# Far-row products as extra matmul columns, near tables from SBUF, and output weights applied last, in a fused attention and convolution kernel

## The chip, the cores and the metric

The kernel runs on one core of a Trainium2 chip. The core has a matrix engine (TensorE, PE, with its weight loads as PEld), a vector engine (VectorE, DVE), a scalar engine with function tables (ScalarE, ACT), a small general engine (GpSimd, POOL), and queues that start DMA transfers, nearly all of them on SyncE (SP). SBUF is the working memory of 128 partitions; PSUM is the memory of eight banks into which PE writes its sums. The metric is the device time of one execution in microseconds; lower is better.

## The reference

Two independent halves are put side by side in the output. Half A is linear attention with 16 heads of 28 features, on 2048 rows of width 448. Half B is a long convolution of a signal `u` (2048 x 448) with a kernel made of 256 complex exponentials for each channel.

```python
# A
q, k, v = split(x @ wqkv)                                # 16 heads of 28
phi_q = concat(softmax(q @ w_phi), softmax(-(q @ w_phi)))  # the same for k
kv, z = phi_k^T @ v, sum(phi_k)
a = ((phi_q @ kv) / (phi_q . z + 1e-6)) @ wo
# B
dt = exp(log_dt);  P = exp(dt * (A_re + 1j*A_im) * l)    # l = 0..2047, rounded to bf16
K = real(sum_n C * P * dt * B)                           # (448, 2048)
y = irfft(rfft(u, 4096) * rfft(K, 4096))[:2048] + u * Dskip
out = concat([a, y], axis=-1)
```

## The kernel before, in words

The kernel first builds a list of about a thousand operations (`Prog.add`), each for one engine: E is PE, A is ACT, V is DVE, G is GpSimd, S is SP. Four lists written into the file then settle everything else. `ORDER` gives the order in which the operations are issued, and so the order on each engine; `PLACES` gives each buffer its address in SBUF; `SLOTS` gives each matmul group its PSUM banks; `PICKS` says for each movable copy, scaling or square (`either`, line 200) whether ACT or DVE does it. Each engine works strictly in its order. Nothing is chosen at run time.

**Half B** is worked on in four quarters `qt` of 112 channels. Because l is rounded to bf16, only 640 different positions l occur, and each is a high part `HI` (16 values, step 16) plus a low part `LO` (40 values). `tables(qt)` (line 789) makes the powers of the exponentials: `rotations` (sines and cosines) and `dampings` (exponentials) take their angles from PSUM, where `args` (line 454) has multiplied them by 1, 3, 5 and 7 on PE; `damp` multiplies the two into 14 near rows of the table `W`; `far` (line 499) makes the 24 far rows out of the near ones by complex products with the 256th power (`step`: two products, one difference, one sum) and by squaring (`squares`); `hi_tables` makes the table `U_` of the high parts by repeated complex products. `build_k` (line 552) then forms the kernel at all positions by matmuls of `U_` (32 columns of weights, four column groups side by side) with `W` (80 moving columns), and `scatter_k` brings the result into the layout of the spectrum by a round trip through DRAM (`KTd`).

The spectrum of the signal is made by `signal_spectrum` (line 406) for two blocks of 1024 rows. It needs the sum and the difference of the even rows and the reversed odd rows; the reversal is a matmul with `REV`, copied out of PSUM. `kernel_spectrum` does the same for the kernel; its second block also takes the first block's result (`sk0`) as a moving operand, and its copy out of PSUM permutes the columns. `conv(qt)` multiplies the spectra (`prod`, on DVE), adds up real and imaginary parts either on DVE (`finish`) or on PE (`finish_pe`, for the blocks named in `ON_PE`), and goes back by `inverse` (line 764): four groups of nine matmuls of 112 columns in a bank, one of the nine for Dskip, then a copy and a store.

**Half A**: `key_side` (line 594) forms exponentials of the keys for 8 pairs of row blocks, their sums (`bz`), reciprocals, the weighted values `VR` and the products `kv`; at its end it transposes `kv` and multiplies it with the output weights `wo` into `M`. `query_side(sc)` (line 637), four times, forms the queries' exponentials, the denominators, scales the exponentials with them and multiplies with `M` (eight matmuls for each 128 rows).

A few helpers issue almost everything, so most rows of the profile carry a helper's line: 177 is any two-operand DVE instruction, 194 a reciprocal, 198 an activation with a function, 205 a copy, 208 a scaling, 211 and 212 a square, 220 a matmul, 230 a transpose, 240 a DMA, 236 a DMA with transpose.

## Time and profile before

| | |
|---|---|
| runs shown, us | 238.6, 238.61, 236.22; median 238.6 |
| span of the profiled execution | 233.5 us |
| between the span and a run's time | 2.7 to 5.1 us; the profiled execution's own time is not shown apart from its span |
| PE busy | 208.1 us (89%), 3044 matmuls |
| DVE busy | 216.8 us (93%), 267 instructions |
| ACT busy | 183.9 us (79%), 321 instructions |
| POOL busy | 4.6 us |
| DMA | 36.4 MB in 81640 packets |

A busy time is that in which at least one instruction of the engine is under way; instructions of one engine overlap a little, so the sum of their durations is larger. Matmuls are pipelined, and a busy PE is not PE at its peak. The granted clock of TensorE was 1.000 over the span.

### The profile page before, as it was taken

The page shows a single profiled execution, that of the slowest core. Times are in us where ns is not written, and L with a number is a line of the kernel's source. Part 1 is how long each engine was busy: PE and PEld are TensorE (multiplying, and loading weights), DVE is VectorE, ACT ScalarE, POOL GpSimd, SP SyncE. Part 2 cuts the span into 40 slices and gives each one's busy share as a digit, 9 for nine tenths or more (in the row PEclk, how much of TensorE's full clock was granted, in tenths as well). Part 3 has the DMA queues.
Part 4 walks back from the last instruction along what each step waited for, and adds up shares of the span by engine and source line. Part 5 has one row for each costly group of instructions (what it writes and reads, how often), then busy time and mean ns, then how long its engine had stood idle before and what let it go on. Part 6 is the DMA issues. An engine that isn't in the chain of part 4 may idle for free.

```text
span 233.5 us, 7103 instructions
## 1 busy us (share of the span) xinstructions
PE 208.1 (89%) x3044; PEld 152.8 (65%) x3044; DVE 216.8 (93%) x267; ACT 183.9 (79%) x321; POOL 4.6 (2%) x20
## 2 busy tenths in 40 slices
PE   1173899998999999999987999999999999999994
PEld 1161446564557655589765678885579968689993
DVE  1799999999999999989999979999999999999980
ACT  3999999999999999999998998698328451355331
POOL 4000000000000100000000000000000000000000
PEclk9999999999999999999999999999999999999999
DMA  5999910499239999826865899872696890489643
GB/s 154 237 218 272 151 37 1 167 150 235 71 59 190 147 176 257 152 71 155 206 156 144 99 255 225 226 114 61 70 368 131 199 277 10 63 185 242 121 100 81
DMA packets 81640, 36.40 MB, mean 156 GB/s; under 512 B 65480, under 2 KB 79688, under 8 KB 81224
## 3 DMA queue, kind: packets, MB, share of 16 engines
q1 hardware_dynamic: 81368, 35.71, 73.3%
q8 instruction: 24, 0.39, 0.7%
q10 hardware_dynamic: 240, 0.23, 0.3%
q14 instruction: 8, 0.07, 0.1%
HBM read 19.44 MB, written 8.62 MB: 120 GB/s over the span
## 4 chain that ended last, share of the span: by engine, by line
PE 51%; ACT 17%; DVE 13%; DMA 5%; issue 3%; SPq 0%; ACTq 0%
PE psum L220 51%; DVE sbuf L177 11%; ACT sbuf L198 8%; ACT sbuf L205 7%; DMA sbuf<-sbuf 3%; DMA sbuf<-KTd 2%; ACT L198 1%; DVE sbuf L205 1%; DVE sbuf L194 0%; ACT sbuf L211 0%; SPq L240 0%; DVE sbuf L212 0%; ACT sbuf L208 0%; DVE sbuf L208 0%; PE psum L230 0%
## 5 line engine op out<-in xcount | busy, mean ns | idle before, releaser
L220 PE MATMUL psum<-sbuf 128*128 128x112 bf16 (+9 forms) x3000 | 206.2, 252 | 21.4 <-ACT sbuf L205 7.8
L177 DVE TENSOR_TENSOR sbuf<-sbuf 128x896 bf16<-128x896 bf16 (+11 forms) x222 | 197.3, 956 | 7.2 <-ACT sbuf L198 4.3
L220 PEld LDWEIGHTS <-sbuf 128*128 128x128 bf16 (+3 forms) x3000 | 150.1, 114 | 75.3 <-issue 18.2
L205 ACT CAST sbuf<-psum 128x448 bf16<-128x448 f32 (+4 forms) x129 | 79.7, 672 | 38.0 <-PE psum L220 37.3
L198 ACT ACTIVATE sbuf<-psum 128x448 bf16<-128x448 f32 (+4 forms) x110 | 65.5, 721 | 0.5 <-PE psum L220 0.4
L211 ACT ACTIVATE sbuf<-sbuf 128x896 bf16<-128x896 bf16 x14 | 14.2, 1024 | 4.0 <-DVE sbuf L177 4.0
L198 ACT ACTIVATE sbuf<-psum,sbuf 128x896 f32<-128x896 f32 (+3 forms) x17 | 13.6, 835 | 0.0
L208 ACT ACTIVATE sbuf<-sbuf 128x896 bf16<-128x896 bf16 (+2 forms) x10 | 10.9, 1091 | 1.4 <-DVE sbuf L299 0.8
L198 ACT ACT_TABLE_LOAD x8 | 10.3, 1283 | 1.4 <-PEq L900 1.3
L205 ACT COPY sbuf<-sbuf 128x224 bf16<-128x224 bf16 (+2 forms) x18 | 8.9, 512 | 0.0
L205 DVE CAST sbuf<-psum 128x448 bf16<-128x448 f32 (+3 forms) x8 | 5.3, 690 | 2.3 <-PE psum L220 1.7
L215 POOL MEMSET sbuf<- 128x224 bf16 (+4 forms) x15 | 4.2, 314 | 153.3 <-PE psum L220 153.1
L205 ACT COPY sbuf<-psum 112x896 bf16<-112x896 bf16 (+2 forms) x13 | 6.8, 549 | 0.1
L177 DVE TENSOR_TENSOR sbuf<-psum,sbuf 128x448 bf16<-128x448 f32 (+3 forms) x12 | 5.1, 444 | 0.1
L194 DVE RECIPROCAL sbuf<-psum 128x64 bf16<-128x64 f32 x8 | 4.3, 546 | 0.4 <-ACT sbuf L198 0.3
L230 PEld LDWEIGHTS <-sbuf 112*112 112x112 bf16 (+1 forms) x44 | 3.1, 128 | 1.8 <-DVE sbuf L177 0.8
L230 PE MATMUL psum<-sbuf 112*112 112x112 bf16 (+1 forms) x44 | 3.6, 215 | 0.6 <-DVE sbuf L177 0.6
L212 DVE TENSOR_TENSOR sbuf<-sbuf 128x896 bf16<-128x896 bf16 (+1 forms) x3 | 3.3, 1087 | 0.0
L194 DVE RECIPROCAL sbuf<-sbuf 128x64 f32<-128x64 f32 x4 | 2.2, 545 | 0.0
L189 DVE SCALAR_TENSOR_TENSOR sbuf<-sbuf 128x64 f32<-128x64 f32 (+1 forms) x5 | 2.0, 393 | 0.0
L205 ACT CAST sbuf<-sbuf 128x1792 bf16<-128x1792 f32 x1 | 1.8, 1814 | 0.0
L208 DVE TENSOR_SCALAR sbuf<-sbuf 128x1568 bf16<-128x1568 bf16 (+1 forms) x3 | 1.6, 538 | 0.0
(8 smaller groups left out, 2.1 us busy)
## 6 DMA issues: line engine op xcount, KB each, us to landing
SUd<-sbuf SPq DMA_DIRECT2D x8, 448.0 KB
sbuf<-SCd SPq DMA_DIRECT2D x16, 224.0 KB
sbuf<-SUd SPq DMA_DIRECT2D x4, 896.0 KB
sbuf<-const SPq DMA_DIRECT2D x3, 1024.0 KB
sbuf<-const SPq DMA_DIRECT2D x8, 384.0 KB
sbuf<-in_B_u_dram SPq DMA_DIRECT2D x4, 448.0 KB
out_dram<-sbuf SPq DMA_DIRECT2D x4, 448.0 KB
out_dram<-sbuf SPq DMA_DIRECT2D x16, 112.0 KB
```

The lines of the kernel that those rows point to most:

```text
L177: prog.add("V", lambda: nc.vector.tensor_tensor(out=o, in0=a, in1=b, op=op))
L189: prog.add("V", lambda: nc.vector.scalar_tensor_tensor(out=o, in0=a, scalar=s, in1=b, op0=op0, op1=op1))
L194: nc.vector.reciprocal(o, a)
L198: prog.add("A", lambda: nc.scalar.activation(o, a, fn, **kw))
L205: either(lambda: nc.scalar.copy(o, a), lambda: nc.vector.tensor_copy(o, a))
L208: either(lambda: nc.scalar.activation(o, a, ACT.Copy, scale=s), lambda: nc.vector.tensor_scalar_mul(o, a, s))
L211: either(lambda: nc.scalar.activation(o, a, ACT.Square), lambda: nc.vector.tensor_tensor(out=o, in0=a, in1=a, op=ALU.mult))
L212: lambda: nc.vector.tensor_tensor(out=o, in0=a, in1=a, op=ALU.mult))
L215: prog.add("G", lambda: nc.gpsimd.memset(o, v))
L220: nc.tensor.matmul(o, lhsT=l, rhs=r, **kw)
L230: nc.tensor.transpose(o, i, idn)
```

## The change

- **Near tables.** The angles stay in SBUF in fp32, in one part instead of two bf16 parts; `args` is gone. `rotations` and `dampings` issue 14 activations of 224 columns each, with the multiple as the activation's scale.
- **Far rows.** A complex product of a far row is split in two: the products with the real part are written to the far row, and the products with the imaginary part are written to one of 12 new rows of `W` (40 to 51, `X`) as they are. `build_k` takes 104 moving columns instead of 80, and one addition at the end of `tables` adds the two results. Three of the first seven far rows and two of the next four are still added up on DVE. The squares lose the factor two, which `GROWN` puts into the constant table of the spectrum.
- **High tables.** The last step adds the two products of the imaginary part at once instead of one difference and one sum.
- **Reciprocals** are Ln followed by Exp(-x) on ACT, from a table that holds both; ACT loads that table wherever it goes from sines to exponentials.
- **Signal.** `turn_u` writes the odd rows in reversed order to DRAM (`URd`), from where `load_u` reads them; the reversal matmuls and their copies are gone.
- **Column order.** The signal matmuls read their moving operand in permuted order, the copy of the kernel spectrum is plain, and the inverse writes its 112 columns permuted to PSUM (every other element, in runs of seven).
- **Output weights last.** `M` is gone; a query multiplies with `kv` into a numerator (`NT`, four groups of two matmuls of 512 columns), copies it, and multiplies with `wo` (four matmuls for each 128 rows).
- The second block of quarter 2 sums on PE as well (`ON_PE`).
- `ORDER`, `PLACES`, `SLOTS` and `PICKS` are new from beginning to end.

```diff
 N_LO = 40
 N_HI = 16
+N_W = 52
 QC = 224
 NCOL = 4 * QC
-ODD = [1, 3, 5, 7]
-LO = [0, 8] + [s * p for p in (2, 4, 6, 1, 3, 5, 7) for s in (-1, 1)]
-LO += [256 + p for p in LO[0:8]]
-LO += [2 * LO[i] for i in (16, 18, 19, 21)]
+MULT = (6, 4, 2, 3, 1, 5, 7)
+LO = [0, 8] + [s * p for p in MULT for s in (-1, 1)]
+LO += [256 + LO[i] for i in (0, 7, 6, 5, 4, 3, 2, 1)]
+LO += [2 * LO[i] for i in (16, 17, 18, 19)]
 LO += [256 + p for p in LO[24:28]]
-LO += [2 * LO[i] for i in (24, 26, 28, 30)]
+LO += [2 * LO[i] for i in (24, 25, 28, 29)]
...
+GROWN = [1, 1, 1, 2, 8]
+ON_PE = [(0, 1), (1, 1), (2, 1)]
...
+            F[blk, kt, r] += GROWN[kt] * np.stack([even.real, odd.real, even.imag, odd.imag])
...
-    def recip(o, a):
-        def fn():
-            with nc.allow_low_precision(reason="bf16 softmax weights, as in the reference"):
-                nc.vector.reciprocal(o, a)
-        prog.add("V", fn)
+    def recip(o, a, ln):
+        af(ln, a, ACT.Ln)
+        af(o, ln, ACT.Exp, scale=-1.0)
 
     def af(o, a, fn, **kw):
-        prog.add("A", lambda: nc.scalar.activation(o, a, fn, **kw))
+        def do():
+            kind = {ACT.Sin: "sin", ACT.Exp: "exp", ACT.Ln: "exp"}.get(fn)
+            if kind == "exp" and prog.kind != "exp":
+                nc.scalar.preload_act_table_set("natural_log_exp_and_others")
+            prog.kind = kind or prog.kind
+            nc.scalar.activation(o, a, fn, **kw)
+        prog.add("A", do)
 
...
+    ue = [sb([128, 4, D_MODEL]) for _ in range(2)]
+    uo = [sb([128, 4, D_MODEL]) for _ in range(2)]
+
+    def turn_u():
         rs = u2.ap[0][0]
-        return bass.AP(tensor=u2.tensor, offset=u2[row + 128 * (1 - a), 0].offset,
-                       ap=[[2 * rs, 64], [256 * rs, 4], [1, 2 * D_MODEL]])
-
-    ua = [sb([128, 4, 2, D_MODEL]) for _ in range(2)]
+        dma("S", URd.rearrange("(g i) d -> g i d", g=16),
+            bass.AP(tensor=u2.tensor, offset=u2[127, 0].offset, ap=[[128 * rs, 16], [-2 * rs, 64], [1, D_MODEL]]))
 
     def load_u(b):
+        rs = u2.ap[0][0]
         for a in range(2):
-            dma("S", ua[b][64 * a:64 * a + 64].rearrange("p t r d -> p t (r d)"), row_pairs(1024 * b, a))
+            p = slice(64 * a, 64 * a + 64)
+            dma("S", ue[b][p], bass.AP(tensor=u2.tensor, offset=u2[1024 * b + 128 * (1 - a), 0].offset,
+                                       ap=[[2 * rs, 64], [256 * rs, 4], [1, D_MODEL]]))
+            src = URd[64 * (8 * b + 6 + a), 0:1]
+            dma("S", uo[b][p], bass.AP(tensor=src.tensor, offset=src.offset,
+                                       ap=[[D_MODEL, 64], [-128 * D_MODEL, 4], [1, D_MODEL]]))
 
...
-            sub(o1, i, o0)
+            copy(view(dst[:, 56 * nch:56 * nch + 1], [112, 8], [1, 2], [2, 28]),
+                 view(psum[:, b[nch], 0:1], [56, 8], [28, 2], [1, 28]))
...
-        ab = sb([128, 2, 4, D_MODEL])
-        ur = sb([128, 4, D_MODEL])
-        for tp in range(2):
-            bs = prog.banks(2)
-            mms([(psum[:, bs[k], 0:D_MODEL], REV, ua[b][:, 3 - 2 * tp - k, 1, :], dict(start=True, stop=True))
-                 for k in range(2)])
-            copy(ur[:, 2 * tp:2 * tp + 2, :], two(bs))
-        add(ab[:, 0], ua[b][:, :, 0, :], ur)
-        sub(ab[:, 1], ua[b][:, :, 0, :], ur)
+        ab = (ue[b], sb([128, 4, D_MODEL]))
+        sub(ab[1], ue[b], uo[b])
+        add(ue[b], ue[b], uo[b])
...
+                                     [(G1[:, cp, jt, 128 * mt:128 * mt + 128], view(ab[cp ^ st][:, jt, 0:1], [14, 32], [1, 2], [2, 7]))
...
     def rotations(qt):
         T = sb([128, 2, 7, QC])
-        p0, far_ = args(TH, qt)
-        for n, f, r0, step in ANGLES:
-            for c_ in range(2):
-                t0 = T[:, c_, r0, 0:1]
-                if n == 4:
-                    dst, src = [view(t, [s, 2], [QC, 2], [1, QC]) for t, s in ((t0, 2 * QC), (p0, far_))]
-                elif n == 2:
-                    dst, src = [view(t, [s, 2], [1, QC]) for t, s in ((t0, step * QC), (p0, QC))]
-                else:
-                    dst, src = T[:, c_, r0, :], view(p0, [1, QC])
-                af(dst, src, ACT.Sin, scale=float(f), **(dict(bias=bias_hp) if c_ == 0 else {}))
+        for c_ in range(2):
+            for r, m in enumerate(MULT):
+                af(T[:, c_, r, :], TH[:, qt * QC:qt * QC + QC], ACT.Sin, scale=float(m), **(dict(bias=bias_hp) if c_ == 0 else {}))
         return T
 
     def dampings(qt):
         A = sb([128, 21, QC])
-        p0, far_ = args(AT, qt)
-        for n, f, r0, step in ANGLES:
-            for sgn in (1, -1):
-                r = 3 * r0 + (sgn > 0)
-                w0 = A[:, r, 0:1]
-                if n == 4:
-                    dst, src = [view(t, [s, 2], [c, 2], [1, QC]) for t, s, c in ((w0, 6 * QC, 3 * QC), (p0, far_, QC))]
-                elif n == 2:
-                    dst, src = [view(t, [s, 2], [1, QC]) for t, s in ((w0, step * 3 * QC), (p0, QC))]
-                else:
-                    dst, src = A[:, r, :], view(p0, [1, QC])
-                af(dst, src, ACT.Exp, scale=float(sgn * f))
+        for i in range(2):
+            for r, m in enumerate(MULT):
+                af(A[:, 3 * r + i, :], AT[:, qt * QC:qt * QC + QC], ACT.Exp, scale=float((2 * i - 1) * m))
         return A
 
-    def damp(W, A, T, qt, x0, w):
-        scaled(A[:, 2:21:3, x0:x0 + w], A[:, 1:20:3, x0:x0 + w], -1.0)
...
+    def far(W, qt):
+        X = W[:, :, N_LO:N_W, :]
+
+        def times_far(o, s0, d, n):
+            mul(o, view(W[:, 1, s0, 0:1], [-WS, 2], [d * QC, n], [1, QC]),
+                view(P256[:, 0, qt * QC:qt * QC + 1], [NCOL, 2], [0, n], [1, QC]))
+
+        def step(s0, d, d0, n):
+            mul(view(W[:, 0, d0, 0:1], [WS, 2], [1, n * QC]), view(W[:, 0, s0, 0:1], [WS, 2], [d * QC, n], [1, QC]),
+                view(P256[:, 2, qt * QC:qt * QC + 1], [0, 2], [0, n], [1, QC]))
+
+        def plus(d0, n, t):
+            o = W[:, :, d0:d0 + n, :]
+            add(o, o, t)
 
         def squares(s0, ka, kb, d0):
             def four(part, row, a, b):
+                return view(W[:, part, row, 0:1], [a * QC, 2], [b * QC, 2], [1, QC])
+            sq = [sb([128, 4, QC]) for i in range(2)]
             for i in range(2):
+                af(sq[i].rearrange("p (a b) x -> p a b x", a=2), four(i, s0, ka, kb), ACT.Square, scale=HALF)
             mul(four(1, d0, 2, 1), four(0, s0, ka, kb), four(1, s0, ka, kb))
+            sub(W[:, 0, d0:d0 + 4, :], sq[0], sq[1])
+        for part in range(2):
+            copy(W[:, part, 16, :], P256[:, 2 - part, qt * QC:qt * QC + QC])
+        step(7, -1, 17, 7)
+        t = sb([128, 2, 3, QC])
+        times_far(t, 7, -1, 3)
+        plus(17, 3, t)
+        times_far(X[:, :, 0:4, :], 4, -1, 4)
+        squares(16, 2, 1, 24)
+        step(24, 1, 28, 4)
+        times_far(X[:, :, 4:8, :], 24, 1, 4)
+        plus(28, 2, X[:, :, 4:6, :])
+        mset(X[:, :, 4:6, :], 0.0)
+        squares(24, 4, 1, 32)
+        step(32, 1, 36, 4)
+        times_far(X[:, :, 8:12, :], 32, 1, 4)
...
+        def part_times(i, z):
+            mul(t[:, :, :, i, :], U_[:, :, 0:8, 1 - i, :],
+                z.rearrange("p (s x) -> p s x", x=28).unsqueeze(2).to_broadcast([128, 8, 8, 28]))
+        part_times(0, N128[:, cols])
+        part_times(1, PW[128][:, 1, cols])
+        times(U_[:, :, 8:16], U_[:, :, 0:8], PW[128][:, 0, cols], 16)
+        add(U_[:, :, 8:16], U_[:, :, 8:16], t)
...
+                        items.append((view(psum[32 * g:32 * g + 32, b, j:j + 1], [nj, 2 * N_W]),
+                                      view(W[:, ri, 0, x:x + 1], [QC, N_W], [1, 2]),
...
+            recip(view(VR[:, 0, 0, D_HEAD, 0:1], [(D_HEAD + 1) * 16, 4], [1, 16]),
+                  psum[:, bz, 0:64].rearrange("p (a h) -> p a h", a=4), LN)
...
-        for ip in range(4):
-            mms([(psum[0:112, b[k], 0:D_MODEL], KVT[:, 2 * ip + k, :], wo[:, (2 * ip + k) % 4, :],
...
+        EQ8 = EQ.rearrange("p s c t -> p (s c) t")
+        mul(EQ8, EQ8, SB)
+        NT = sb([112, 4, 512])
+        for c in range(4):
+            (b,) = prog.banks(1)
+            mms(acc(psum[0:112, b, :], [(KVN[:, s, c].rearrange("p h d -> p (h d)"), EQ[:, s, c, :]) for s in range(2)]))
+            copy(NT[:, c, :], psum[0:112, b, :])
...
-            mms(acc(psum[:, b, 0:D_MODEL], [(EQ[:, i // 4, i % 4, 128 * t4:128 * t4 + 128], M[:, i, :])
-                                            for i in range(8)]))
+            mms(acc(psum[:, b, 0:D_MODEL], [(NT[:, c, 128 * t4:128 * t4 + 128], wo[:, c, :]) for c in range(4)]))
...
-            items.append((view(o[:, 0:1], [14, 8], [7, 2], [1, 7]), (NEG, ident)[cp],
-                          view(sk0(1 - cp, m)[:, 0:1], [14, 8], [1, 2], [2, 7]), dict(start=False, stop=True)))
+            items.append((o, (NEG, ident)[cp], sk0(1 - cp, m), dict(start=False, stop=True)))
...
-                copy(view(sk[:, b, 0, m // 4, m % 4, 0:1], [896, 2], [14, 16], [2, 7], [1, 2]),
-                     view(psum[:, bk, 0:1], [224, 2], [14, 16], [1, 7], [7, 2]))
+                copy(view(sk[:, b, 0, m // 4, m % 4, 0:1], [896, 2], [1, 224]), view(psum[:, bk, 0:1], [224, 2], [1, 224]))
...
-                    items += acc(psum[:, bk, 112 * jt:112 * jt + 112],
+                    items += acc(view(psum[:, bk, 112 * jt:112 * jt + 1], [14, 8], [1, 2], [2, 7]),
                                  [(GI[:, r, cp, mt, 128 * jt:128 * jt + 128], S[:, r, cp, 112 * mt:112 * mt + 112])
-                                  for cp in range(2) for mt in range(4)] + [(UT[:, b, r, 128 * jt:128 * jt + 128], DD[:, qt, :])])
+                                  for cp in range(2) for mt in range(4)] + [(UT[:, b, r, 128 * jt:128 * jt + 128], view(DD[:, qt, 0:1], [14, 8], [1, 2], [2, 7]))])
...
+        add(*(2 * [view(TS[:, 20, 0:1], [8 * 28, 3], [1, 4 * 28])]), TS[:, N_LO:N_W, :].rearrange("p (a l) x -> p a (l x)", a=3))
```

159 lines of the change are left out of this document (55 added, 104 removed), and 107 rows, old and new, of tables (ORDER, PLACES, SLOTS).

## The prediction

> **What bounds the kernel now.** I read the page first: the span, the engines' shares, the slices and the chain. Slices are 5.8 us each.
>
> ```profile
> span 233.5 us, 7103 instructions
> PE 208.1 (89%) x3044; PEld 152.8 (65%) x3044; DVE 216.8 (93%) x267; ACT 183.9 (79%) x321; POOL 4.6 (2%) x20
> ...
> DVE  1799999999999999989999979999999999999980
> ACT  3999999999999999999998998698328451355331
> ...
> DMA  5999910499239999826865899872696890489643
> GB/s 154 237 218 272 151 37 1 167 150 235 71 59 190 147 176 257 152 71 155 206 156 144 99 255 225 226 114 61 70 368 131 199 277 10 63 185 242 121 100 81
> ...
> PE 51%; ACT 17%; DVE 13%; DMA 5%; issue 3%; SPq 0%; ACTq 0%
> ```
>
> The reader sees three nearly full engines. ACT is full to about slice 22 and then thins out; DVE is full nearly throughout. I then asked for the busy time in four stretches (us, then the busy time of PE, weight loads, DVE and ACT, instructions in brackets, the clock, the DMA share, GB/s). The first cut, 157.5, is the end of the third quarter's table matmuls (`build_k`).
>
> ```profile
> 10.00:157.50 147.50, 133.89 (x1842) 92.40 (x1842) 144.53 (x191) 143.31 (x250) 1.58 (x6) 1.00 0.78 158
> 157.50:230.10 72.60, 72.56 (x1200) 58.91 (x1190) 68.78 (x71) 33.90 (x66) 0.51 (x2) 1.00 0.69 151
> 30.00:130.00 100.00, 94.02 (x1216) 62.09 (x1214) 98.41 (x136) 98.68 (x176) 1.58 (x6) 1.00 0.68 138
> ```
>
> So there are two stages. In stage 1 (to 157.5) DVE and ACT have together no slack: 144.5 and 143.3 of 147.5 us. In stage 2 (157.5 to 230.1) PE never pauses, DVE is busy 68.8 of 72.6, ACT under half. After 230.1 come a last copy and its store, 3.4 us. The clock stands at 1.00 throughout.
>
> **Prices.** Group rows give a mean and a busy time; for DVE I use busy time over count. (The last figure of a row after the bar is the mean in ns.)
>
> ```profile
> L177 DVE TENSOR_TENSOR sbuf<-sbuf 128x3584 bf16<-128x3584 bf16 x23 | 46.1, 2020 | 0.1
> L177 DVE TENSOR_TENSOR sbuf<-sbuf 128x1792 bf16<-128x1792 bf16 x44 | 46.1, 1081 | 0.0
> L177 DVE TENSOR_TENSOR sbuf<-sbuf 128x896 bf16<-128x896 bf16 x74 | 43.0, 617 | 2.3 <-ACT sbuf L211 1.8
> L177 DVE TENSOR_TENSOR sbuf<-sbuf 128x3136 bf16<-128x3136 bf16 x16 | 28.2, 1783 | 0.4 <-ACT sbuf L205 0.4
> L177 DVE TENSOR_TENSOR sbuf<-sbuf 128x1568 bf16<-128x1568 bf16 x8 | 7.5, 957 | 0.0
> L194 DVE RECIPROCAL sbuf<-psum 128x64 bf16<-128x64 f32 x8 | 4.3, 546 | 0.4 <-ACT sbuf L198 0.3
> L177 DVE TENSOR_TENSOR sbuf<-psum,sbuf 128x448 bf16<-128x448 f32 x4 | 2.5, 649 | 0.0
> L220 PE MATMUL psum<-sbuf 128*128 128x224 bf16 x64 | 8.9, 291 | 5.2 <-DMA sbuf<-const 4.7 <-ACT sbuf L198 0.5
> L198 ACT ACTIVATE sbuf<-psum 128x896 bf16<-128x896 f32 x12 | 11.8, 1020 | 0.0
> L198 ACT ACTIVATE sbuf<-psum 112x512 bf16<-112x512 f32 x32 | 18.8, 729 | 0.0
> L198 ACT ACT_TABLE_LOAD x8 | 10.3, 1283 | 1.4 <-PEq L900 1.3
> L205 ACT COPY sbuf<-sbuf 128x224 bf16<-128x224 bf16 x8 | 3.5, 456 | 0.0
> L205 ACT CAST sbuf<-psum 128x320 bf16<-128x320 f32 x7 | 4.0, 598 | 4.0 <-PE psum L220 4.0
> ```
>
> ACT instructions overlap their neighbours, so their cost is the time from start to start. The chain has four 448-wide exponentials in 1.76 us, 0.44 each; the timeline has a 224-wide copy from SBUF at 26.00, the next instruction at 26.28 and another copy at 26.62. That is 0.28 for a 224-wide instruction without a bias and 0.34 for one with it, about 0.18 below the mean; 896 from PSUM then costs 0.82, 512 about 0.5.
>
> ```profile
> 66.73 1.76 ACT sbuf L198 x4
> 160.94 12.11 PE psum L220 x64
> ...
> 26.00 0.55 ACT L205 COPY sbuf<-sbuf 128x224 bf16<-128x224 bf16 x1
> 26.28 0.62 ACT L198 ACTIVATE sbuf<-psum,sbuf 128x224 bf16<-128x224 f32 x1
> 26.62 0.55 ACT L205 COPY sbuf<-sbuf 128x224 bf16<-128x224 bf16 x1
> ```
>
> On PE, 64 matmuls of 448 columns take 12.11 us, 0.189 each.
>
> **DVE, part by part.** A quarter's far rows cost 2x3136, 2x1568, 4x1792 and 8x896 elements: 3.5+1.9+4.2+4.6 = 14.2. After: one 3136, two 1344 (0.82, an estimate between its neighbours), five 1792, five 896 and one small add at the end: 11.9. Four quarters give -9.4. Twelve reciprocals at 0.54 go to ACT: -6.5. The four subtractions that split an angle in two bf16 parts: -2.5. Conv 2's second block sums on PE, so one 3584 and four 896 go: -4.3. The last step of `hi_tables` trades two 1792 and one 3584 for two 1792 and one 3584: zero. The new pick string puts more copies on DVE (four 896-wide from PSUM or SBUF, five more 448-wide from PSUM, one 1792, eight of 224): +8. Together about -14.7 of 216.8.
>
> **ACT.** The angles: 48 activations from PSUM (16 each of 896, 448, 224: 13.1+7.0+4.1 = 24) become 112 of 224 from SBUF at 0.30: +9.6. 24 short Ln and Exp at about 0.11: +2.6. The new 16 numerator copies of 512: +7.7. Gone: seven scalings by two (-6), eight copies of 896 for the reversal and the folded output weights (-6.4), two of eight table loads (the new order changes function six times, five of them in stage 1, where all eight lie before: -2.6 in all), copies given to DVE (-8). Two more squares and table copies of 416 for 320 elements: +3.7. Together about +0.6.
>
> **PE.** Gone: 64 angle matmuls at half of 0.189 (-6.1), 8 reversals (-1.5), 8 transposes and 8 weight products (-1.9), half of the 128 output matmuls (-12.1). New: 32 of 512 columns (+6.9), 32 of 448 for conv 2 (+6.0). That is -8.7. Three layouts are unknown prices:
>
> ```profile
> 153.28:157.49 4.21, 4.21 (x224) 4.21 (x224) 4.21 (x9) 4.18 (x8) 0.00 (x0) 1.00 0.50 143
> 211.62:213.76 2.14, 2.14 (x46) 2.14 (x43) 2.11 (x4) 1.27 (x3) 0.00 (x0) 1.00 0.99 323
> 226.62:228.06 1.44, 1.44 (x34) 1.44 (x31) 0.18 (x1) 0.47 (x1) 0.00 (x0) 1.00 0.46 104
> ```
>
> The first row is one quarter's `build_k`: 224 matmuls of 80 columns in 4.21 us, 75 ns for each four that run side by side. With 104 columns the price lies between 0 and 30%, 0 to +5; I take +4.4, since 75 ns is over twice what 80 columns take at the 448-wide rate, so columns decide. The other two rows, less four matmuls in flight at their starts, give 51 ns for a bank's second half and 48 for the inverse; every third matmul of the former reads every other element (`sk0`), so such a read costs about +9 ns per 112 columns. The 128 signal matmuls now read so, 448 columns each: 0 to +4.6, taken at +4.6. (`sk0` loses what the Dskip matmuls gain.) Last, all 576 inverse matmuls write every other PSUM element. The only strided writes of the trace are `build_k`'s, at 75/80 = 0.94 ns per column against 0.43: between 0 and (105-48) ns x 576 = +33 us. I take 0: those matmuls also read in pairs from far-apart rows, and a read price of the `sk0` kind accounts for them without one for the write. PE comes out at about +0.3.
>
> **New waits.** The key side's products now wait for Ln and Exp in ACT's queue instead of a reciprocal on DVE itself; DVE's table work is queued behind them: 0 to 8 x 0.3 = +2.4, taken at 0, because the new order puts table work between. The output of a query passes one more copy on ACT between two matmul groups; PE has the next kernel spectrum behind it and ACT is idle half of stage 2, so 0 there (16 x 0.5 = 8 if every one were waited for). GpSimd clears 896 elements a quarter, about 1 us, with squares and two products beside it on DVE: 0.
>
> **Start.** `turn_u` writes 0.9 MB of the signal to DRAM in reversed order and reads it back, in the slices where the DMA row shows 9: at the page's 272 to 151 GB/s some 4 us of traffic ahead of the weights on SP's queue, which also issues four loads of u more. DVE's subtraction, in the new order right behind the first C copy, waits for the round trip, and the powers and the whole table work are queued behind it on DVE. Against it, the signal matmuls need no reversal first and can start some us before the 27.03 of now.
>
> ```profile
> 27.03 1.47 PEld L220 LDWEIGHTS <-sbuf 128*128 128x128 bf16 x8 [0.17 <-issue]
> ```
>
> Price -2 to +3, taken at +0.5.
>
> **The sum.** I count instructions of both order lists up to the third `build_k` and after it, at start-to-start prices. Stage 1: DVE 147 to 139.5 (-7.7), ACT 145.4 to 140.5 (-4.9), PE 126 to 126. Stage 2: DVE 68.8 to 62.4, PE 68.8 to 69.2. Stage 1 is limited by DVE and ACT alike, so I take the middle, -6.3, and +0.5 for the start. Stage 2 is PE's: the DVE time it loses is worth nothing there, and PE gains 0.4. So the span is 233.5-6.3+0.5+0.4 = 228.1. The runs shown lie 2.7 to 5.1 us above this span, the median at the upper end: 228.1+5.1 = 233. The ends move with the two engines of stage 1: 229 to 237.
>
> **Rivals.**
> *The permuted write halves the inverse's rate (slower).* If the write is what makes `build_k` slow, 576 matmuls cost +25 (rate halved) to +33, nearly all in stage 2 where PE has no slack: 233+25 = 258 and more. It decides from about 10 ns per matmul (5.8 us), which eats the gain. For it: no strided write in the trace is fast. Against: the pairwise read explains the same row. [...]
> *ACT becomes the bound of stage 1 (no change).* If the 112 short activations cost the group row's 3.5/8 = 0.44, not 0.30, ACT gets +13 over the 95 or so that fall in stage 1: 238.6-4.9+13 = 247 at worst, and 240 at half that. Against: the three timeline rows. [...]
> *DVE alone decides.* If the new order also removes PE's 6% of pauses between 30 and 130, so that PE runs ahead and stage 2 shrinks with DVE, the whole 13 to 15 us come off: 225.
> *The start waits.* If the reversed signal lands late, +3 to +5 at once: 236 to 238.
>
> **Chances.** About 2.4 us (1%) is what a measurement here can tell from nothing, so faster means under 236.2 and slower over 241. Forecast 0.48 (0.42 of it under 236.2); DVE alone 0.17; the late start or ACT around 240 0.15, with 0.04 of it over 241; the permuted write 0.20. So faster 0.59, same 0.17, slower 0.24. The range leaves out the permuted write and the tip of the best case: 222 to 246; the forecast's own range is 229 to 237.
>
> **What would show it.**
>
> ```profile
> 228.33 0.53 ACT L205 CAST sbuf<-psum 128x448 bf16<-128x448 f32 x1 [1.24 <-PE psum L220]
> 230.10 0.53 ACT L205 CAST sbuf<-psum 128x448 bf16<-128x448 f32 x1 [1.24 <-PE psum L220]
> ```
>
> Right: `build_k` near 5.2 us a quarter, banks of the inverse still 1.77 us apart at the end, as the last two copies are now, third `build_k` done near 151, table loads six, near-table activations 0.3 apart, PE without pauses in stage 2. Wrong: inverse banks 3 us apart; ACT busier than now up to the third `build_k`; DVE idle before 20 us on a DMA; PE pausing in stage 2.

## The result: 12.6% slower, and the profile after

The changed kernel takes 267.4 us (median of four, 266.8 to 268.2) against 237.4 us for the kernel before: a ratio of 1.126 with a 95% interval of 1.118 to 1.134. The forecast was 233 us, a gain, with a range of 222 to 246; the kernel is slower, and its time lies above that range. Medians here are of all executions, while a ratio and its interval leave out those more than 1.5% above the fastest of their kernel, so small differences below are read from the ratios. The profiled execution has a span of 265.3 us, 31.8 more than before.

First the page of the changed kernel: span, busy time per engine, the slices of PE, DVE and ACT, and the shares of the chain of waits.

```profile
span 265.3 us, 6993 instructions
PE 234.2 (88%) x2956; PEld 174.6 (66%) x2956; DVE 205.5 (77%) x250; ACT 186.0 (70%) x398; POOL 8.0 (3%) x24
...
PE   1145999996897989999998989999999999999994
...
DVE  1469999999998689999979996999996481179400
ACT  3797989899999699999998979985532402131021
...
PE 50%; DVE 6%; ACT 6%; DMA 5%; issue 3%; SPq 1%; DVEq 0%; ACTq 0%
```

DVE has 11.3 us less to do than before, ACT 2.1 more, and PE 26.1 more, with 88 matmuls fewer. The slices (6.6 us each) say where: the last third is all nines on PE, with holes in DVE and ACT.

The same in stretches (us, then the busy time of PE, weight loads, DVE and ACT): the first ends with the third quarter's `build_k`, the second with the last matmul.

```profile
10.00:161.90 151.90, 133.32 (x1759) 87.31 (x1758) 139.64 (x177) 141.42 (x317) 4.77 (x12) 1.00 0.74 152
161.90:261.80 99.90, 99.83 (x1200) 86.34 (x1192) 64.28 (x69) 39.09 (x76) 1.30 (x3) 1.00 0.55 117
```

Stage 2 grew from 72.6 to 99.9 us, and PE never pauses in it. Stage 1 ends at 161.9 instead of 157.5, although DVE (139.6 for 144.5) and ACT (141.4 for 143.3) have less to do. Two things went wrong, then: a large one in stage 2, and a gain in stage 1 that did not come. The groups by line and form show the large one, the 112-column matmuls, first before, then after:

```profile
L220 PE MATMUL psum<-sbuf 128*128 128x112 bf16 x1064 | 55.4, 213 | 4.0 <-ACT sbuf L205 2.6 <-DMA sbuf<-KTd 1.5
```

```profile
L227 PE MATMUL psum<-sbuf 128*128 128x112 bf16 x1064 | 82.1, 260 | 0.4 <-ACT sbuf L204 0.4
```

As many matmuls of the same size take 26.7 us more. Of the 1064, the 576 of the inverse are those whose output pattern changed. The last copies of inverse banks, the view that the prediction named as its test, show 3.45 us from bank to bank (258.32 to 261.77) where it was 1.77:

```profile
258.32 0.53 ACT L212 CAST sbuf<-psum 128x448 bf16<-128x448 f32 x1 [2.44 <-PE psum L227]
261.77 0.53 ACT L212 CAST sbuf<-psum 128x448 bf16<-128x448 f32 x1 [2.92 <-PE psum L227]
```

36 matmuls in 3.45 us are 96 ns each; before, 1.77 us for 36 were 49.

### The profile page after: what moved, and what is told of

It is laid out like the page before. It is cut to its first block, busy times and chain, and to the rows that moved or that the text cites. A ratio compares the mean times of both kernels' runs of the same rounds, so it can differ in the third digit from the quotient of the medians.

```text
span 265.3 us, 6993 instructions
## 1 busy us (share of the span) xinstructions
PE 234.2 (88%) x2956; PEld 174.6 (66%) x2956; DVE 205.5 (77%) x250; ACT 186.0 (70%) x398; POOL 8.0 (3%) x24
## 4 chain that ended last, share of the span: by engine, by line
PE 50%; DVE 6%; ACT 6%; DMA 5%; issue 3%; SPq 1%; DVEq 0%; ACTq 0%
PE psum L227 50%; DVE sbuf L180 6%; DMA sbuf<-SCd 5%; ACT sbuf L204 4%; ACT sbuf L212 2%; SPq L247 1%; DVE sbuf L212 0%; DVEq L180 0%; PE psum L237 0%; ACTq L212 0%
## 5 line engine op out<-in xcount | busy, mean ns | idle before, releaser
L227 PE MATMUL psum<-sbuf 128*128 128x112 bf16 (+8 forms) x2920 | 232.9, 276 | 26.9 <-DVE sbuf L180 9.4
L227 PEld LDWEIGHTS <-sbuf 128*128 128x128 bf16 (+3 forms) x2920 | 172.6, 122 | 84.7 <-issue 17.6
L180 DVE TENSOR_TENSOR sbuf<-sbuf 128x896 bf16<-128x896 bf16 (+13 forms) x205 | 186.8, 966 | 25.2 <-ACT sbuf L212 9.4
L204 ACT ACTIVATE sbuf<-sbuf 128x224 bf16<-128x224 f32 (+4 forms) x145 | 61.2, 495 | 5.3 <-DVE sbuf L180 3.2
L204 ACT ACTIVATE sbuf<-psum 112x512 bf16<-112x512 f32 (+3 forms) x82 | 45.6, 673 | 2.4 <-PE psum L227 1.7
L212 DVE CAST sbuf<-psum 128x448 bf16<-128x448 f32 (+1 forms) x9 | 6.9, 773 | 11.9 <-PE psum L227 11.9
L222 POOL MEMSET sbuf<- 128x224 bf16 (+5 forms) x19 | 7.5, 427 | 182.0 <-DVE sbuf L180 85.9
L212 ACT COPY sbuf<-sbuf 128x224 bf16<-128x224 bf16 (+2 forms) x13 | 5.6, 474 | 1.6 <-DVE sbuf L180 1.6
L212 ACT COPY sbuf<-psum 128x128 f32<-128x128 f32 (+2 forms) x11 | 5.0, 465 | 0.2 <-PE psum L237 0.2
L204 ACT ACTIVATE sbuf<-psum,sbuf 128x896 f32<-128x896 f32 x5 | 4.9, 1003 | 0.0
```

The costliest lines, as they stand in the source:

```text
L180: prog.add("V", lambda: nc.vector.tensor_tensor(out=o, in0=a, in1=b, op=op))
L204: nc.scalar.activation(o, a, fn, **kw)
L212: either(lambda: nc.scalar.copy(o, a), lambda: nc.vector.tensor_copy(o, a))
L222: prog.add("G", lambda: nc.gpsimd.memset(o, v))
L227: nc.tensor.matmul(o, lhsT=l, rhs=r, **kw)
```

## The experiments

### The strided write

**The inverse writes in a row, everything else as changed.** The permutation moves into the copy that empties the bank.

```diff
-items += acc(view(psum[:, bk, 112 * jt:112 * jt + 1], [14, 8], [1, 2], [2, 7]),
+items += acc(psum[:, bk, 112 * jt:112 * jt + 112],
...
-copy(OB.rearrange("p t x -> p (t x)"), psum[:, bk, 0:D_MODEL])
+copy(view(OB[:, 0, 0:1], [14, 32], [1, 2], [2, 7]), view(psum[:, bk, 0:1], [14, 32], [7, 2], [1, 7]))
```

> The changed kernel with one edit: the inverse matmuls write their 112 PSUM elements in a row, and the copy that empties the bank puts the columns in order. Theory 1 (the write of every other PSUM element costs the inverse half its rate: 96 ns from start to start in the changed kernel against 49 before): 576 matmuls times 47 ns is 27 us, nearly all where PE is the bound, so about 241 us, the inverse back at 49 ns, the last two banks 1.8 us apart. Rival A (the matmuls slowed down for another reason, such as the order in which they come or the strided read of their last operand): 262 us or more. Rival B (the write is slow, but something else is late next): 245 to 258 us, with PE pausing in the last 100 us.

Measured: 241.3 us, ratio to before 1.014 (1.002 to 1.026). Theory 1 holds: about 26 us of the 30 that were lost are this write. First lines of the page, the two stages, and the last two banks:

```profile
span 236.5 us, 6994 instructions
...
PE 207.8 (88%) x2956; PEld 148.2 (63%) x2956; DVE 205.9 (87%) x250; ACT 188.8 (80%) x398; POOL 8.0 (3%) x24
```

```profile
10.00:159.00 149.00, 133.28 (x1760) 87.33 (x1759) 139.19 (x177) 141.48 (x317) 4.77 (x12) 1.00 0.74 156
...
159.00:232.70 73.70, 73.49 (x1198) 60.00 (x1188) 64.97 (x70) 41.66 (x75) 1.30 (x3) 1.00 0.69 153
```

```profile
230.94 0.77 ACT L212 CAST sbuf<-psum 128x448 bf16<-128x448 f32 x1 [0.38 <-PE psum L227]
232.74 0.77 ACT L212 CAST sbuf<-psum 128x448 bf16<-128x448 f32 x1 [1.03 <-PE psum L227]
```

Banks are 1.80 us apart again, although the Dskip matmuls still read their operand with a step, so that read is not the cause. The permuting copy costs 0.77 us instead of 0.53, on an engine that is idle there. PE's busy time, 207.8, is that of before less 0.3; stage 2 is 73.7 us long, 1.1 more than before.

**The same write alone, in the kernel before.** Nothing else of the change is in it; the copy reads the bank back in order.

```diff
-items += acc(psum[:, bk, 112 * jt:112 * jt + 112],
+items += acc(view(psum[:, bk, 112 * jt:112 * jt + 1], [14, 8], [1, 2], [2, 7]),
...
-copy(OB.rearrange("p t x -> p (t x)"), psum[:, bk, 0:D_MODEL])
+copy(OB.rearrange("p t x -> p (t x)"), view(psum[:, bk, 0:1], [14, 32], [1, 2], [2, 7]))
```

> The kernel before with one edit: the inverse matmuls write every other PSUM element and the copy that empties the bank reads them back in order. Nothing else of the change is in it. Theory 1: 576 times 47 ns, of which stage 2 has no slack for any: 262 to 265 us. Rival A: no change, 237 to 240 us.

Measured: 261.7 us, ratio 1.106 (1.096 to 1.117). Its group row is like that of the changed kernel, and 82.3 less the 55.4 of before is 26.9 us:

```profile
L220 PE MATMUL psum<-sbuf 128*128 128x112 bf16 x1064 | 82.3, 261 | 3.6 <-ACT sbuf L205 2.6 <-DMA sbuf<-KTd 1.0
```

Undone in one kernel and done alone in the other, the edit has one price, 24 to 26 us, nearly all of the 27 us that PE is busy longer: hardly any of it is hidden behind other work.

**Gaps, but pairs kept together.** What is it in the pattern that costs? Here the same matmuls write runs of two elements (8 bytes) with gaps of two.

```diff
-items += acc(view(psum[:, bk, 112 * jt:112 * jt + 1], [14, 8], [1, 2], [2, 7]),
+items += acc(view(psum[:, bk, 112 * jt:112 * jt + 1], [2, 2], [4, 28], [1, 2]),
...
```

> The kernel before, the inverse matmuls writing runs of two elements (8 bytes) with gaps of two between them, read back in order by the copy. [...] If every address that is not in a row costs: like the stride of two, 262 to 265 us and 96 ns. [...]

Measured: 236.4 us, ratio 0.988 (0.976 to 1.000): no slower, where a price on every address that is not in a row would have given 262 to 265. The group row, and the last two banks, again 1.77 us apart:

```profile
L220 PE MATMUL psum<-sbuf 128*128 128x112 bf16 x1064 | 55.6, 213 | 3.0 <-ACT sbuf L205 2.6 <-DMA sbuf<-KTd 0.3 <-DMA sbuf<-const 0.2
...
227.48 0.53 ACT L205 CAST sbuf<-psum 128x448 bf16<-128x448 f32 x1 [1.24 <-PE psum L220]
229.25 0.53 ACT L205 CAST sbuf<-psum 128x448 bf16<-128x448 f32 x1 [1.24 <-PE psum L220]
```

So gaps as such cost nothing here: 49 ns per matmul with results in pairs and gaps between the pairs, as with all 112 in a row. With the step of two elements, where consecutive results lie next to each other only between the runs of fourteen, it is 96 ns. Every pair of this run starts at an even element of its bank; pairs that start at an odd one were not tried.

### What build_k costs

**build_k writes its columns in a row** (on top of the first edit; the copy to `TS` reads strided).

```diff
-items.append((view(psum[32 * g:32 * g + 32, b, j:j + 1], [nj, 2 * N_W]),
+items.append((psum[32 * g:32 * g + 32, b, 2 * N_W * j:2 * N_W * j + 2 * N_W],
...
```

> The first edit, and build_k also writes its 104 columns in a row (the copy to TS reads them in the strided order instead). Theory 1, same cause in build_k: its 106 ns for each four matmuls falls towards the plain rate of 0.43 ns per column, 45 to 55 ns, so 11 us less PE time over the four quarters, of which 3 lie where PE alone is the bound and the others beside DVE and ACT: 231 to 238 us, a quarter's build_k 3.0 to 3.5 us. Rival (the read of pairs from rows far apart is what costs): build_k stays at 106 ns and the time at that of the first edit.

Measured: 241.0 us (ratio 1.016, 1.002 to 1.030): no change from 241.3. Theory 1, that the write is what makes `build_k` slow too, falls. Two windows of the fourth quarter, each with 160 of its matmuls behind one another (us, then the busy times): the kernel of the first edit, with the strided write, and this one, in a row. Four take 94 to 95 ns in both.

```profile
194.63:198.41 3.78, 3.78 (x161) 3.78 (x160) 3.78 (x6) 2.15 (x4) 0.00 (x0) 1.00 0.02 4
```

```profile
196.30:200.10 3.80, 3.80 (x162) 3.80 (x160) 3.80 (x6) 2.17 (x4) 0.00 (x0) 1.00 0.02 4
```

**build_k reads one row instead of pairs from rows far apart.** The edit makes another product; there is one execution (237.3 us), which gives no verdict on the time but a trace. It stands on top of the column order of before (next section).

```diff
-view(W[:, ri, 0, x:x + 1], [QC, N_W], [1, 2]),
+view(W[:, ri, 0, x:x + 1], [1, 2 * N_W]),
```

> As the run with old columns, and build_k reads its 104 moving columns from one row (104 elements next to each other) instead of 52 pairs from rows 448 bytes apart, so that its product is another. Writing PSUM in a row changed nothing. Theory (the read of pairs is what makes four matmuls take 106 ns): 45 to 60 ns for each four, a quarter about 3 us. Rival (four matmuls on four column groups of the array are paced by something else, such as the loads of their weights): 106 ns as before.

```profile
194.14:197.63 3.49, 3.49 (x160) 3.49 (x160) 3.49 (x5) 1.97 (x4) 0.00 (x0) 1.00 0.02 5
```

3.49 us for 160 are 87 ns for each four, against 94 with the pairs (3.78): the read is worth 7 ns. So neither the write nor the read explains why four matmuls of 104 columns on four column groups take twice what one takes at the plain rate (104 x 0.43 = 45 ns, an estimate from the inverse's 48 ns for 112). What paces them stays open. The time goes with the columns: 75 ns for 80 before and 94 for 104 are 0.94 and 0.91 ns per column, which a fixed cost of loading weights would not give. (The 106 ns in the expectations are the mean with the pauses at bank changes in it.)

**build_k with 80 columns**, on the same base; the 12 rows of second products are left out of the product.

```diff
-view(W[:, ri, 0, x:x + 1], [QC, N_W], [1, 2]),
+view(W[:, ri, 0, x:x + 1], [QC, N_LO], [1, 2]),
...
```

> As the run before last (old columns), and build_k multiplies 80 columns as in the kernel before; the 12 rows of far second products are computed by DVE but left out of the product, and the copy to TS reads twelve rows twice so that it stays as long. Theory (four matmuls of 104 columns take 106 ns, of 80 columns 75): 7 us less PE time in all, 1.7 us of it where PE is the bound, the rest next to pauses: 2 to 5 us less than with old columns alone. Rival (build_k is paced by its weight loads or by the copies): 106 ns for each four stay, and the time does too.

Measured: 237.7 us, ratio 1.002 (0.997 to 1.007), against 1.010 (1.005 to 1.015) on its base. PE's busy time falls by 6.7 us (4.7 of it in `build_k`'s own group row, 24.6 to 19.9), the time by 1.5 by the medians and 2 by the ratios. That is about the 1.7 us expected in stage 2; most of what was saved in stage 1 did not arrive.

```profile
PE 199.9 (85%) x2956; PEld 144.4 (61%) x2956; DVE 205.2 (87%) x250; ACT 185.2 (79%) x398; POOL 8.0 (3%) x24
```

### The column order as a whole

**The column order of before in the changed kernel**: the signal's matmuls read in a row, the kernel's spectrum is put in order in its copy, the inverse and its copy are plain (the lines of the inverse are left out here).

```diff
-view(ab[cp ^ st][:, jt, 0:1], [14, 32], [1, 2], [2, 7]))
+ab[cp ^ st][:, jt, :])
...
-copy(view(sk[:, b, 0, m // 4, m % 4, 0:1], [896, 2], [1, 224]), view(psum[:, bk, 0:1], [224, 2], [1, 224]))
+copy(view(sk[:, b, 0, m // 4, m % 4, 0:1], [896, 2], [14, 16], [2, 7], [1, 2]),
+     view(psum[:, bk, 0:1], [224, 2], [14, 16], [1, 7], [7, 2]))
```

> The changed kernel with the column order of before all through: the signal's matmuls read their 448 columns in a row, the kernel's spectrum is put in order in its copy as before, the inverse writes in a row, the output copy is plain. The first edit alone gave 241.3 us. Theory (the strided read costs 221 against 189 ns on each of 128 signal matmuls, 4.1 us of PE time in the first half, where PE, DVE and ACT all pause now and then): 237 to 240 us. Rival (that PE time is covered by DVE and ACT): as with the first edit, 241 us. A bank of the signal matmuls takes 189 ns per matmul in either case.

Measured: 239.2 us, ratio 1.010 (1.005 to 1.015). The signal's matmuls went from 221 to 189 ns from start to start, 4.1 us for the 128 at that difference; against the first edit's 1.014 the time is not told apart. This kernel is the base of the following; its page has these busy times:

```profile
PE 206.6 (86%) x2956; PEld 149.1 (62%) x2956; DVE 205.1 (86%) x250; ACT 185.9 (78%) x398; POOL 8.0 (3%) x24
```

### The start

**No reversed copy of the signal in DRAM** (the odd rows come unreversed, so the spectrum is not that of the signal).

```diff
-            src = URd[64 * (8 * b + 6 + a), 0:1]
+            src = u2[1024 * b + 128 * (1 - a) + 1, 0:1]
...
-    turn_u()
```

> As the run before (old columns), and the reversed copy of the signal in DRAM is left out: the odd rows come straight from the input, not reversed, so the spectrum is not that of the signal; all sizes and all other instructions stay. Theory (what stage 1 lost is DVE's start, which waits 2.2 us for these rows at 17 us, with the powers queued behind): 3 to 5 us less than the run before. Rival (the sines that the powers need come at 17.5 us because ACT runs the near exponentials first, so DVE waits anyway): within 1.5 us of the run before.

Measured: 238.3 us, ratio 1.009 (1.005 to 1.012), against 1.010 of the base: 1 us by the medians, less by the ratios, so the rival holds and a gain is not told from none. DVE's first sums begin without a wait, at 16.97 us instead of 18.28 on the base.

**The signal turned later**, the reversal behind the loads of A, B and C, DVE's two sums and the first signal matmuls behind the first power and the square. Only the order list changed.

> As the run with old columns, with only the order changed: the signal is turned behind the loads of A, B and C on the sync queue, and DVE's subtraction and sum of the two signal halves, and the first signal matmuls, come after the first power and the square of stage 1. Theory (the start costs 3 to 5 us because DVE's first powers are queued behind the signal's rows): 2 to 4 us less than with old columns alone. Rival (the sines come late, not the rows): no gain, or 1 to 2 us lost because the signal matmuls start later.

Measured: 245.2 us, ratio 1.038 (1.031 to 1.045), 6 us slower: the opposite of the theory. DVE's first power comes 5 us earlier than on the base (19.27 for 24.35 us), as the theory had it, and that gains nothing. The two sums begin at 27.08, with no wait for the rows, and PE, which has nothing but the signal's matmuls to do, stands for 13 us until 29.34:

```profile
29.34 10.89 PE L227 MATMUL psum<-sbuf 128*128 128x448 bf16 x48 [13.22 <-DVE sbuf L180]
```

PE's delay comes back to DVE through ACT's fixed order: ACT's copy of the first signal bank waits 6.39 us for PE, until 32.41, the near-table activations are queued behind it, and DVE then waits for ACT:

```profile
35.46 4.96 DVE L180 TENSOR_TENSOR sbuf<-sbuf 128x1792 bf16<-128x1792 f32 x3 [4.11 <-ACT sbuf L204]
```

So what counts in the start is when PE gets the signal more than when DVE gets to the first power.

### Which engine sets stage 1

The forecast took the mean of what DVE and ACT lose there. The following runs take work from one engine, or add it, on the base of 239.2 us.

**One sum back from PE to DVE** (third group, second block): `ON_PE` loses `(2, 1)`, and the lists of order, banks and picks follow.

> As the run with old columns (239.2 us), with one more part of the change undone: the second output block of the third conv group is summed by DVE again (one sum of 3584 and four of 896 elements, about 4.2 us of DVE time) instead of by 32 matmuls of 448 columns on PE (6.0 us at 189 ns) and two copies. Theory (stage 2 is PE's, DVE has 8 us of slack there): 233 to 236 us. Rival (the DVE sums come late in the last 25 us, where the last group's sums are queued behind them, and PE waits): 238 to 242 us.

Measured: 240.1 us, ratio 1.011 (1.006 to 1.017), the base's 1.010; the rival holds. PE's busy time falls to 200.0 us, but its chain now runs through DVE shortly before the end (start, length, what):

```profile
217.26 5.14 DVE sbuf L180 x7
...
223.04 2.04 DVE sbuf L180
...
225.10 2.04 DVE sbuf L180
...
229.04 3.71 PE psum L227 x72
```

**Less DVE work**: on the kernel with 80 columns in `build_k`, two of the three far second products of a quarter are computed for 2 elements.

> As the run with old columns and 80 columns in build_k (237.7 us), and two of the three far second products of each quarter, which build_k does not read there, are computed for 2 elements instead of 1792: 8 x 0.95 = 7.6 us less DVE time, 5.7 us of it up to the third build_k. The kernel's far rows are not those of the reference. Theory (DVE still sets stage 1): 232 to 234 us. Rival (stage 1 is set by the start and by one engine waiting for the other in the order of the list, DVE being idle 18 of its 159 us): 236 to 238 us.

Measured: 236.8 us, ratio 0.997 (0.993 to 1.001), against 1.002 without this edit: 1 us, within the intervals, for 5.7 us of DVE time in stage 1 (198.1 for 205.2 us busy in all).

**More ACT work**: the seven cosine rows of each quarter are issued twice.

> As the run with old columns (239.2 us), and seven of the 28 near-table activations of each quarter are issued twice in a row: 28 x 0.287 = 8.0 us more ACT time, 6 to 8 us of it up to the third build_k, and no other engine has more to do. Theory (ACT sets stage 1): 245 to 247 us. Rival (ACT's idle time of 12 us in stage 1 takes it): 239 to 241 us.

Measured: 252.1 us, ratio 1.063 (1.059 to 1.068). The 28 more activations carry a bias, and with them ACT is busy 13.2 us longer than on the base, not the 8.0 of the expectation. 12.9 were paid, nearly all of it.

```profile
PE 209.1 (83%) x2956; PEld 149.7 (60%) x2956; DVE 206.2 (82%) x250; ACT 199.1 (79%) x426; POOL 8.0 (3%) x24
```

**Less ACT work, by GpSimd**: the same rows filled with a constant.

```diff
+if c_ == 0:
+    mset(T[:, c_, r, :], 0.5)
+else:
```

> As the run with old columns (239.2 us), with the seven cosine rows of each quarter's near tables filled with a constant by GpSimd instead of computed by ACT, so that the tables are not the reference's: 28 x 0.38 us = 10.6 us less ACT time, up to the third build_k or soon after. The run with as many issued twice cost 12.9 us. Theory (ACT sets stage 1 after the start): 229 to 232 us. Rival (ACT, DVE and PE are so near each other that the next one takes over at once): 235 to 238 us.

Measured: 241.4 us, ratio 1.021 (1.014 to 1.027): no gain, 2 us lost, with ACT busy 9.3 us less (176.6). Its DVE and GpSimd timelines show a side effect: a copy of 1792 elements, 1.08 us long on the base, takes 3.77 while sixteen memsets run: they began first and end at 26.12, and it ends at 27.07, about one length of its own later. Whether this is where the 2 us went was not tried.

```profile
23.30 3.77 DVE L212 CAST sbuf<-sbuf 128x1792 bf16<-128x1792 f32 x1
...
22.44 3.68 POOL L222 MEMSET sbuf<- 128x224 bf16 x16 [19.88 <-DVE sbuf L180]
```

What makes the copy wait these rows do not show.

**Work moved from ACT to DVE**, ten operations within SBUF, then six copies from PSUM as well (letters of the pick string).

> As the run with old columns (239.2 us), with ten copies and one of the scalings within SBUF (one of 1568, three of 448, six of 224 elements) moved from ACT to DVE: 4.5 us less on ACT by its start-to-start times (1.41, 0.46, 0.28), 2.6 us more on DVE (0.54, 0.30, 0.20). Theory (ACT sets stage 1): 3 to 5 us less, 234 to 236 us. Rival (DVE takes over): 238 to 240 us.

> As the run before, and six of the copies of V from PSUM (448 elements: 0.42 us on ACT, 0.54 on DVE) move to DVE as well: another 2.5 us less on ACT, 3.2 us more on DVE. Theory (ACT still sets stage 1): another 1 to 2.5 us less. Rival (DVE is the bound of the stretch from 50 to 110 us by then): as the run before, or up to 2 us more.

Measured: 240.7 us (ratio 1.012, 1.004 to 1.020) and 242.9 us (1.025, 1.019 to 1.032). ACT is busy 3.7 and 6.0 us less, DVE 2.0 and 5.4 more (207.1 and 210.5). The first leaves the time where it was (base 1.010); the second costs about 3.6 us, so work added to DVE is paid as well, and the second run's rival holds.

**Less ACT work without GpSimd; less DVE work; both, and no round trip.** Their tables are not the reference's. The cosines of a quarter come from one activation; three sums in place per quarter are left out.

> As the run with old columns (239.2 us), and the seven cosine rows of a quarter come from one activation of 1568 elements (all seven with multiple 1, so the tables are not the reference's): 4 x (7 x 0.38 - 1.41) = 5.0 us less on ACT, nothing more on GpSimd, whose memsets had stopped a DVE copy for 2.7 us in the earlier run with less ACT work. Theory 1 (ACT alone sets stage 1): 234 to 236 us. Theory 2 (DVE sets the pace from 18 to 58 us, ACT's key-side exponentials after that, and PE and both between; what one engine saves is lost in a wait for another): 238 to 240 us.

> As the run with old columns (239.2 us), and three sums in place per quarter are left out of DVE's work (3584, 1344 and 896 elements: 1.94 + 0.77 + 0.54 = 3.2 us a quarter, so that tables and far rows are not the reference's): 9.7 us less DVE time up to the third build_k. A theory that DVE alone sets stage 1: 230 to 233 us. Theory 2 (shared): 237 to 239 us, as taking 5.7 us off DVE gave 1.

> The two runs before together, and without the reversed copy of the signal in DRAM (the odd rows come unreversed): 5.0 us less on ACT, 9.7 us less on DVE up to the third build_k, DVE's start about 1 us earlier. Theory 2 (shared: only together do the savings reach the end): 229 to 233 us, clearly more than the sum of the single ones. A rival theory 3 (PE, with its pauses, is the bound of stage 1): 236 to 238 us.

Measured: 242.0 us (ratio 1.012, 1.001 to 1.024), 238.6 us (1.011, 1.004 to 1.017) and 239.3 us (1.012, 1.003 to 1.021). None gained on the base's 1.010, nor did all together: theory 2, by which the savings reach the end only together (229 to 233 us), falls. Theory 3, that PE with its pauses bounds stage 1 (236 to 238 us), comes nearest and is not excluded. With everything taken out, this is what the chain of waits looks like from 99 us on, and what the engines did in three stretches (window, then PE, weight loads, DVE, ACT, GpSimd, and the granted clock):

```profile
99.26 16.04 PE psum L228 x317
...
119.33 6.47 DMA sbuf<-SCd
...
128.64 8.53 DMA sbuf<-SCd
...
139.63 2.51 PE psum L228 x20
...
142.20 90.03 PE psum L228 x1507
```

```profile
0.00:30.00 30.00, 11.16 (x68) 7.04 (x69) 19.21 (x21) 23.93 (x38) 1.90 (x9) 0.89 0.98 218
30.00:142.00 112.00, 103.80 (x1333) 68.47 (x1332) 97.79 (x138) 103.20 (x230) 3.70 (x10) 0.98 0.66 137
142.00:232.30 90.30, 90.21 (x1558) 73.50 (x1556) 75.50 (x80) 54.35 (x108) 2.37 (x5) 1.00 0.72 155
```

From 142 us on PE runs 90 us without a pause. Before that no engine is full: DVE has 14 us free of the 112, ACT and PE 8 to 9. The granted clock was 0.89 and 0.98 in the first two stretches, so PE may have been slower there; but at clocks of 0.976 to 0.978 the base took 238.4 and 239.2 us and this kernel 237.5, 238.9 and 239.7, so the clock does not hide a gain of the size that was expected. From 115 us to 142 the chain is one of latencies, of which the transfers of the scores (`SCd`, 6.5 and 8.5 us) are the longest; none of the edits touches them. Whether they, or the order in which PE's work stands, set the 142 us was not tried and stays open.

## Why the prediction was wrong, point by point

- **The step that failed: the inverse's strided write, taken at 0.** Its bound was right (0 to +33 us), and its rival was priced at 258 us and more, with a chance of 0.20; the runs put the price at 24 to 26 us, 96 ns for each of the 576 matmuls in place of 49. The reading behind it was that `build_k`'s slow row shows a write price or a read price, and that the read accounts for it. The runs show that it shows next to nothing of either: with the write in a row or strided it takes 94 to 95 ns for each four, with another read 87. The row had no bearing on the inverse, so it could not argue for 0. What remained was a price from 0 to +33 us that no row of the trace told, and 0 was its lower end. With the write undone the time is 241.3 us, inside the wide range and still above the forecast's own 229 to 237.
- **Stage 1, taken at -6.3, came out at about +1.5** (157.5 to 159.0 us with the strided write undone), the second failure and the other 8 us. The terms were too large: between 10 us and the end of the third `build_k`, DVE's busy time fell by 5.3 us (7.7 forecast) and ACT's by 1.8 (4.9 forecast). And their idle time in that stretch rose by more, DVE's from 3.0 to 9.8, ACT's from 4.2 to 7.5. The sum of busy times of two nearly full engines was taken for a bound; the runs show that it is not one: work added to ACT or DVE was paid, work removed from any of the three, or from two at once, gave 2 us or less. PE was left out of that bound, though its own count was 126 us before and after. From 30 us to the end of stage 1 it was busy 121.5 of 127.5 us before and 120.7 of 129.0 with the write undone (rows below, before and first edit), so a gain of 6.3 had to come from all of its 6.0 us of pauses there, or from the start. What holds the end of stage 1 in its place instead (the latency of the score transfers, the fixed order of the queues) is argued from the chain and not shown.

```profile
30.00:157.50 127.50, 121.52 (x1770) 84.27 (x1767) 124.70 (x173) 123.37 (x222) 1.58 (x6) 1.00 0.74 150
```

```profile
30.00:159.00 129.00, 120.67 (x1692) 80.43 (x1690) 121.35 (x160) 122.63 (x280) 4.77 (x12) 1.00 0.67 145
```

- **DVE, -14.7**: measured -11.3. The rival in which DVE alone decides fell: 9.7 us less DVE time in stage 1 gave nothing that can be measured.
- **ACT, +0.6**: measured +2.1. The near activations are 0.28 us apart without a bias (ten in 2.89 us) and up to 0.38 with one, near the 0.30 that was taken. ACT is busier by 1.5 us than forecast, not by 13; the rival with 0.44 fell as worked out, though more ACT work does cost.
- **PE, +0.3 without the write**: measured -0.3. The signal's strided read, taken at 4.6, is 4.1 (32 ns x 128). `build_k`, taken at +4.4: 94 ns in an uninterrupted stretch for the 75 of before is 19 ns x 224 = 4.3, and its group rows, which hold the pauses at bank changes, differ by 5.8 (18.3 to 24.1). That the sum came out so close is in part luck: these two terms are off by -0.5 and by up to +1.4.
- **The start, +0.5**: DVE does 18.2 us of work in its first 30 instead of 23.3 (rows below, before and after), 5 us less; a sign that the prediction named came true as well, DVE idle before 20 us on a DMA (2.18 us until 19.27). Yet little of that reaches the end: without the reversal the time is the same within 1 us, near the 0.5 that was taken.

```profile
0.00:30.00 30.00, 14.02 (x90) 9.64 (x91) 23.29 (x26) 26.12 (x36) 2.51 (x12) 1.00 0.95 204
```

```profile
0.00:30.00 30.00, 12.17 (x71) 7.25 (x72) 18.16 (x21) 22.47 (x42) 1.90 (x9) 1.00 1.05 210
...
19.27 4.15 DVE L180 TENSOR_TENSOR sbuf<-sbuf 128x1792 bf16<-128x1792 bf16 x3 [2.18 <-DMA sbuf<-in_B_u_dram]
```

- **The new waits, 0** (the key side's logarithm and exponential, the query's extra copy, GpSimd's clearing): none was tried by itself.
- **Stage 2, +0.4**: +1.1 without the write. That PE does not pause there was right, and it is why the write's price was paid whole. That PE gains there are worth their length was only half right: 6 us less PE work came to nothing when DVE had the sums instead, because they were then late.

## What to carry to other kernels

Let a matmul of the full 128 columns of weights write PSUM so that each two consecutive fp32 results lie side by side, and put a permutation into the copy that empties the bank: here 112 columns took 49 ns in a row or in pairs and 96 with a step of two, 47 more, and there are 36 of those in a bank; the permuting copy cost 0.24 us per bank on an engine with time to spare. `build_k`'s small matmuls showed no such price: four took 94 to 95 ns with the step and in a row. A price bounded from 0 to +33 us by a row that has two explanations is not 0; try to tell the explanations apart. Where three engines are nearly full under a fixed order, less work on one or two of them can come out as idle time there and nothing else (here 9.7 us off DVE, alone or with 5.0 off ACT, gave no gain); compare a gain with the pauses of the engine that keeps its work.

## What the hardware showed that was not expected

- fp32 results of a matmul with a step of two elements: 96 ns for 112 columns against 49; in pairs with gaps: 49.
- Four matmuls of 104 columns on four column groups of 32: 94 ns together, with the PSUM write in a row or strided, 87 when they read one row; 45 is the estimate for one of them at 0.43 ns per column.
- A DVE copy within SBUF took 3.77 us instead of 1.08 while sixteen GpSimd memsets in a row ran, and ended 0.95 us after the last of them.
